# Three projection parts of a tenth set of later tokens move from the segments to the front of a one-core transformer kernel, with its instruction order searched anew

## The chip, the cores and the metric

The kernel runs on one core of a Trainium2 chip. Its engines are TensorE (PE, whose weight loads are listed apart as PEld), VectorE (DVE), ScalarE (ACT), GpSimd (POOL) and SyncE (SP), which issues most of the DMA transfers. The metric is device time in microseconds (us), the median of several runs.

## What is computed

A residual block with two halves, over 2048 tokens of width 640. The first half goes through the tokens in 64 segments of 32. Each segment sees 8 memory rows and its 32 tokens, has 32 heads of width 128, and its first 8 output rows are the memory of the next segment, so segments depend on each other in a chain:

```python
for s in range(n_seg):                       # 64 segments
    h = concatenate([mem, xs], axis=1)       # 8 memory rows + 32 tokens
    q, k, v = h @ Wq, h @ Wk, h @ Wv         # 640 -> 32 heads x 128
    p = softmax(where(mask, q @ k.T * scale, -1e9))
    o = (p @ v) @ Wo                         # 4096 -> 640
    mem = o[:, :M]                           # memory of the next segment
    outs.append(o[:, M:])
h = x + attention(layernorm(x))
out = h + ((relu(g) * u) @ W_down)           # g, u = layernorm(h) @ W_gate, W_up; 1728 wide
```

## The kernel before

**Rows of a segment.** The chain needs 32 rows at a time: 8 of memory and the segment's first 24 tokens. The last 8 tokens of a segment do not depend on memory before attention. They are called the later tokens here (`rest` in the code). They are projected ahead, for four segments at once: 32 rows make a *set*, so there are 16 sets, numbered from 0. A set has six *parts*: Q and K of the first 16 heads, Q and K of the other 16, and V of each half, in the order Q0, K0, Q1, K1, V0, V1. A part is 20 matmuls of 128x512 into one PSUM bank (5 chunks of the contraction, 4 column groups; L1577). Its bank is copied out by ACT (L1411) or DVE (L1412); Q and K are turned by DVE (L1599), K is rearranged by POOL as well (L1604); the result is stored to DRAM (`scr_qk`, L1607; `scr_v`, L1624), and a segment later loads what it needs (`RS`, L1640 and L1644).

**Where the later tokens come from.** Sixteen segments' later tokens, four sets, are loaded, normalized and transposed together (`ln1r`, L1526). Sets 0 to 3 use buffer `xr0`, sets 4 to 7 `xr1`, sets 8 to 11 `xr0` again, filled by a transposing DMA on SP's queue (L1532).

**Stages.** In the first stage Wq, Wk, Wv and Wo are loaded, while PE projects `EARLY` = 9 whole sets and the first segment. Then come the segments. In the gaps of the chain PE does work that is not urgent: the parts of the remaining sets, the output projection of the later tokens (`ro`, L1661), and gate and up projections of the feed-forward part (`gx`, L1742). Last comes the rest of the feed-forward part.

`RATES` says how many parts the segments get: an entry (s0, s1, count) spreads `count` parts over the segments from s0 up to s1. `EXTRA` says how many parts of set number `EARLY` are made in the first stage, with no segment to wait for. The code exists before the change too, with `EXTRA` at 0:

```python
for part in range(EXTRA):
    rest(EARLY, part)
...
for n in range(base + cnt * (s - s0) // (s1 - s0), base + cnt * (s - s0 + 1) // (s1 - s0)):
    z, part = divmod(n + EXTRA, 6)
    z += EARLY
    if z >= NQ:
        break
    rest(z, part, go)
```

In the segments a part also waits for the memory rows of its segment (`go`). Sets from number 8 on use two PSUM banks (4 and 5) and store through SP; the sets before them use all eight and store through ACT. Sets from number 9 on have three staging tiles.

**The order.** The order of each engine's instructions is not written by hand. Each operation is entered with an estimated duration, its dependencies and its buffers. When the kernel is built, a list scheduler (`_Sched.schedule`, L964) plays the program through, and takes, of the operations that can start about now, the one with the highest priority. The priority is the length of the work that follows, plus an entry of the table `BIAS` (L28), by name and by name and segment. The table `ENGINE` (L682) fixes which of ACT and DVE does a copy. Both tables are the result of a search over the scheduler's own model. The instructions then run in this order on each engine, and wait for each other with semaphores. Wherever an engine stands, everything behind it stands too.

**Names that the steps use.** L1577 is every projection (rows `xT` are a segment's own, rows `xr` the later tokens'). L1691 transposes a segment's input rows, of which the memory rows come last: it marks the start of a segment. L1954 and L1958 are scores, L1968 and L1555 sums of the softmax, L1993 and L1998 the product with V, L2027 and L2046 the output projection of the memory rows, L1963 to L1980 the softmax on ACT and DVE, L1497 a normalization, L2076 the turn of a segment's own Q and K, L1778 and L1834 the feed-forward part.

Of the kernel before, what the change touches and what calls it, by code (L numbers as in the profile page):

```python
# [18 lines left out]
RATES = ((1, 20, 32), (20, 50, 10))  # L19
EXTRA = 0  # L20
# [7 lines left out]
BIAS = {"sel2": -428.53, "ezero": 827.13, "ldxs0": 772.6, "ldxs1": -1075.19, "ldxa": 977.15, "ldxl": -444.97,  # L28
    "ldxx": 94.56, "ldxn": 296.11, "ldxx0": -425.81, "ldxst": -946.28, "ldxxm": -329.88, "ldmev": -440.02,
# [18 lines left out]
    "gx": -75.13, "gxrelu": -736.07, "gxev": -228.23, "gxst": -268.67, "ln2nd": -1166.07, "xnld": 1080.06,  # L48
    "gld": -294.56, "gu": 52.5, "relu": 1032.72, "gmul": -789.51, "roz": -16.73, "tn2go": 142.03,
# [1214 lines left out]
def build_kernel(nc, A_x, A_mem0, A_Wq, A_Wk, A_Wv, A_Wo, A_seg_len, B_x, B_W_gate, B_W_up,  # L1264
# [46 lines left out]
    sel2 = ar.alloc("sel2", [128, 64], BF16)  # L1311
# [21 lines left out]
    oTr = [ar.alloc(f"oTr{i}", [128, H, 32], BF16) for i in range(2)]  # L1333
# [547 lines left out]
    for nm, b in (("ldxr", 9000.0), ("ldxr1", 8950.0)):  # L1881
        for t in ("", "s0", "s1", "a", "l", "x", "n", "T", "e"):
            sc.bias[nm + t] = b
# [369 lines left out]
```

## Time and profile before

| | us |
|---|---|
| median of 3 runs | 998.24 |
| lowest and highest run | 994.87, 998.29 |
| profiled execution | 995.62 |
| its span, first to last instruction | 993.9 |

The mean granted clock of TensorE in the profiled execution was 0.998. By the rows of the profile: 21 MB of weights come in during the first stage, each load of Wq, Wk and Wv 512 KB and of Wo 640 KB. The segments last from about 87 us to 874 us, a little over 12 us each.

How to read it: the page gives busy time by engine, the chain of work that ended last, and groups of instructions by line. A row of a group has line, engine, operation, output<-input, shapes and count; then busy time and mean duration in ns; then the idle time of the engine just before and what ended it. A row of the timeline has start and length in us, and in brackets the idle time before it and its releaser. `ps` is a PSUM bank, `stg` and `tok` are staging tiles.

### The profile page before, as it was taken

How to read it: one execution, taken by the hardware profiler on the slowest of the kernel's cores; microseconds unless marked ns; L12 is line 12 of the kernel's file. 1: busy time of each engine (PE TensorE's matmuls, PEld its weight loads, DVE VectorE, ACT ScalarE, POOL GpSimd, SP SyncE). 2: the span in 40 equal slices, each digit the busy share in tenths (PEclk: the TensorE clock that was granted, in tenths of full speed). 3: DMA queues.
4: the chain of work that ended last, by engine and by line, in shares of the span. 5: the costliest groups of instructions: out<-in, count | busy, mean ns of one | idle time of the engine just before them, and what ended most of it. 6: DMA issues, size and time to landing. Idle time of an engine off the chain costs nothing.

```text
span 993.9 us, 54620 instructions
## 1 busy us (share of the span) xinstructions
PE 973.8 (98%) x25518; PEld 535.7 (54%) x24540; DVE 618.3 (62%) x1345; ACT 502.4 (51%) x1226; POOL 112.5 (11%) x264
## 2 busy tenths in 40 slices
PE   7989999999999999999999999999999999999998
PEld 4334565555555555655555556555555565543343
DVE  5835767768676766576666676767656766523232
ACT  2236555556565565555555565555555656521020
POOL 2341011111011011001000010000100000100000
PEclk9999999999999999999999999999999999999999
DMA  8996122223131323232232234333223352289211
GB/s 320 403 350 145 45 57 57 66 53 92 36 89 39 85 76 83 55 81 66 67 84 62 78 105 86 86 93 79 52 72 89 76 102 76 68 260 288 72 41 40
DMA packets 181553, 103.62 MB, mean 104 GB/s; under 512 B 126212, under 2 KB 177484, under 8 KB 181324
## 3 DMA queue, kind: packets, MB, share of 16 engines
q1 hardware_dynamic: 175948, 95.51, 34.5%
q10 hardware_dynamic: 5376, 4.63, 1.4%
q8 instruction: 196, 3.21, 1.3%
q14 instruction: 33, 0.27, 0.1%
HBM read 67.30 MB, written 29.75 MB: 98 GB/s over the span
## 4 chain that ended last, share of the span: by engine, by line
PE 90%; DMA 4%; SPq 3%; DVE 1%; issue 1%; ACT 0%; POOL 0%; ACTq 0%; DVEq 0%; POOLq 0%
PE ps L1577 49%; PE ps L2046 7%; PE ps L1742 7%; PE ps L2027 7%; PE ps L1834 4%; PE ps L1661 3%; PE ps L1778 3%; PE ps L1993 3%; DMA scr_qk<-stg 3%; PE ps L1555 2%; PE ps L1968 2%; PE ps L1954 1%; SPq L2164 1%; DMA Wq<-in_A_Wq_dram 1%; DMA scr_o<-osr 1%
## 5 line engine op out<-in xcount | busy, mean ns | idle before, releaser
L1411 ACT ACTIVATE tok<-ps 128x512 bf16<-128x512 f32 x216 | 128.2, 597 | 146.5 <-PE ps L1577 141.4
L1577 PE MATMUL ps<-Wk,xT 128*32 128x512 bf16 x2560 | 180.4, 379 | 0.4 <-ACT tok L1411 0.4
L1577 PE MATMUL ps<-Wv,xT 128*32 128x512 bf16 x2560 | 176.3, 379 | 0.0
L1577 PE MATMUL ps<-Wq,xT 128*32 128x512 bf16 x2560 | 170.1, 379 | 0.5 <-DVE tok L1412 0.3
L2076 DVE STREAM_TRANSPOSE QT<-tok 128x512 bf16<-128x512 bf16 x128 | 90.6, 708 | 47.5 <-ACT tok L1411 45.4
L1577 PEld LDWEIGHTS ps<-Wq,xT 128*32 128x32 bf16 x2560 | 70.6, 97 | 66.5 <-DVE xT L1691 9.1
L2076 DVE STREAM_TRANSPOSE KT<-tok 128x512 bf16<-128x512 bf16 x128 | 90.8, 709 | 24.6 <-ACT tok L1411 22.7
L1577 PEld LDWEIGHTS ps<-Wk,xT 128*32 128x32 bf16 x2560 | 68.4, 96 | 55.6 <-DVE xT L1691 2.9
L1963 ACT ACTIVATE E<-ps 128x224 bf16<-128x224 f32 x128 | 45.7, 357 | 81.4 <-PE ps L1958 77.7
L2046 PE MATMUL ps<-Wo,oT 128*32 128x160 bf16 x4096 | 83.5, 233 | 1.0 <-issue 1.0
L2046 PEld LDWEIGHTS ps<-Wo,oT 128*32 128x32 bf16 x4096 | 74.1, 97 | 15.5 <-ACT oT L1411 5.6
L2027 PE MATMUL ps<-Wo,oT 128*32 128x320 bf16 x2048 | 81.5, 300 | 0.9 <-DVE oT L1412 0.8
L1577 PEld LDWEIGHTS ps<-Wv,xT 128*32 128x32 bf16 x2560 | 61.0, 96 | 38.8 <-ACT tok L1411 0.7
L1412 DVE CAST oT<-ps 128x320 bf16<-128x320 f32 x124 | 55.0, 485 | 42.9 <-PE ps L1998 36.9
L1940 POOL COPY QT<-RS 128x256 bf16<-128x256 bf16 x64 | 25.7, 402 | 470.4 <-PE ps L1958 470.2
L1411 ACT ACTIVATE Vm<-ps 128x512 bf16<-128x512 f32 x122 | 72.0, 591 | 11.4 <-PE ps L1577 6.3
L1412 DVE CAST tok<-ps 128x512 bf16<-128x512 f32 x104 | 68.7, 661 | 9.6 <-PE ps L1577 9.3
L2027 PEld LDWEIGHTS ps<-Wo,oT 128*32 128x32 bf16 x2048 | 52.7, 96 | 27.3 <-DVE oT L1412 7.7
L1688 DVE CAST_PREDICATED xm<-turn,ps 128x64 bf16<-128x64 uint16 x126 | 27.9, 222 | 61.3 <-PE ps L1555 61.1
L2011 POOL COPY oTr<-oT 128x128 bf16<-128x128 bf16 x128 | 41.0, 320 | 193.5 <-ACT oT L1411 110.4
L1411 ACT ACTIVATE oT<-ps 128x320 bf16<-128x320 f32 x132 | 50.4, 436 | 11.5 <-PE ps L1998 11.1
L1411 ACT ACTIVATE ps<-seed 128x384 f32<-128x384 bf16 x117 | 54.4, 489 | 2.1 <-DVE half L2035 1.8
(108 smaller groups left out, 1453.5 us busy)
## 6 DMA issues: line engine op xcount, KB each, us to landing
RS<-scr_qk SPq DMA_DIRECT2D x63, 128.0 KB, 2.3
big<-in_A_x_dram SPq DMA_DIRECT2D x34, 160.0 KB, 2.8
Wq<-in_A_Wq_dram SPq DMA_DIRECT2D x10, 512.0 KB, 7.7
Wk<-in_A_Wk_dram SPq DMA_DIRECT2D x10, 512.0 KB, 8.2
Wv<-in_A_Wv_dram SPq DMA_DIRECT2D x10, 512.0 KB, 8.6
Wo<-in_A_Wo_dram SPq DMA_DIRECT2D x8, 640.0 KB, 11.2
Wgs<-in_B_W_gate_dram SPq DMA_DIRECT2D x30, 160.0 KB, 3.0
Wus<-in_B_W_up_dram SPq DMA_DIRECT2D x30, 160.0 KB, 2.9
```

What stands on the lines that cost most here:

```text
L1411: return e.activation(dst, src, ACTF.Copy)
L1412: return e.tensor_copy(dst, src)
L1577: o = pe.matmul(out, lhs[c], rhs, start=(c == 0), stop=(c == DC - 1), skip_group_check=True)
L1661: o = pe.matmul(bank(bk)[p0:p0 + 32, 0:2 * SLICE], oTr[b][:, h, :], cols(h, 2 * a, 2 * a + 2), start=(h < 2), stop=(h >= H - 2), skip_grou ...
L1742: o = pe.matmul(bank(bk)[32 * i:32 * i + 32, 0:512], wt[:, c, 32 * i:32 * i + 32], xn2T[0][:, :, c * 128:(c + 1) * 128], start=(c == 0), s ...
L1778: o = pe.matmul(bank(bk)[:, 0:TB], lhs(c), xT[:, :, c * 128:(c + 1) * 128], start=(c == 0), stop=(c == DC - 1))
L1834: pe.matmul(bank(ba)[:, 0:512], lhs, Wd[:, j, 0:512], start=(j == 0), stop=(j == FC - 1), skip_group_check=True)
L1963: op("act", lambda a: a.activation(E[:, g, :, 0:56], sco(BS[g]), ACTF.Exp, scale=SCALE), r=["table"], w=[("E", g)], x=[BS[g]], dur=0.36, n ...
L2011: op("pool", lambda e: e.tensor_copy(oTr[ob][:, 16 * g:16 * g + 16, XR * y:XR * y + XR], oT[:, 16 * g:16 * g + 16, 0:XR]), r=[("oT", g, 0) ...
L2027: o = pe.matmul(bank(BA)[p0:p0 + 32, 0:2 * SLICE], oT[:, h, XR:40], cols(h, 2 * b2, 2 * b2 + 2), start=(i == 0 and jj < 2), stop=(i == 3 a ...
L2046: o = pe.matmul(bank(BW)[32 * j:32 * j + 32, 0:SLICE], oT[:, 16 + 4 * jj + i, XR:40], cols(h, j, j + 1), start=(i == 0 and jj == 0), stop= ...
L2076: op("dve", lambda v, tb=tb, dst=dst: v.transpose(dst, tok[tb.at][:, :].rearrange("p (h r) -> p h r", r=32)), w=[("QT" if p == 0 else "KT" ...
```

## The change

```diff
-RATES = ((1, 20, 32), (20, 50, 10))
-EXTRA = 0
+RATES = ((1, 20, 30), (20, 50, 9))
+EXTRA = 3
...
-BIAS = {"sel2": -428.53, "ezero": 827.13, "ldxs0": 772.6, "ldxs1": -1075.19, "ldxa": 977.15, "ldxl": -444.97,
+BIAS = {"sel2": -751.1, "ezero": 242.82, "ldxrs0": 9232.52, "ldxrs1": 9076.28, "ldxra": 9061.94,
...
-ENGINE = {"ldxre": "act", "ldxr1e": "act", "ldmev": "act", "er0ev": "dve", "er0Tev": "act", "er1ev": "act",
+ENGINE = {"ldxre": "act", "ldmev": "act", "er0ev": "dve", "er0Tev": "act", "er1ev": "act", "ervev": "act",
...
     for nm, b in (("ldxr", 9000.0), ("ldxr1", 8950.0)):
         for t in ("", "s0", "s1", "a", "l", "x", "n", "T", "e"):
-            sc.bias[nm + t] = b
+            sc.bias[nm + t] = BIAS.get(nm + t, b)
```

Three parts of set 9 (Q0, K0 and Q1) are entered with the first stage and wait for no segment. The segments get 39 parts instead of 42. The tables `BIAS` and `ENGINE` are replaced as a whole (of the shared names of `BIAS` none keeps its value), and the first two normalizations of later tokens (`ldxr`, `ldxr1`) may now have entries of their own in place of fixed priorities. No operation is added or removed.

More of the change, by code (lines that the diff above doesn't have):

```diff
@@ L27 @@
 FPIECES = ((512, 896), (896, 1664), (0, 512))
-BIAS = {"sel2": -428.53, "ezero": 827.13, "ldxs0": 772.6, "ldxs1": -1075.19, "ldxa": 977.15, "ldxl": -444.97,
-    "ldxx": 94.56, "ldxn": 296.11, "ldxx0": -425.81, "ldxst": -946.28, "ldxxm": -329.88, "ldmev": -440.02,
[18 rows of a table removed]
-    "gx": -75.13, "gxrelu": -736.07, "gxev": -228.23, "gxst": -268.67, "ln2nd": -1166.07, "xnld": 1080.06,
-    "gld": -294.56, "gu": 52.5, "relu": 1032.72, "gmul": -789.51, "roz": -16.73, "tn2go": 142.03,
[632 rows of a table removed]
-ENGINE = {"ldxre": "act", "ldxr1e": "act", "ldmev": "act", "er0ev": "dve", "er0Tev": "act", "er1ev": "act",
-    "ervev": "act", "r0ev": "dve", "r0Tev": "act", "r1ev": "act", "rvev": "dve", "Q0ev": "act", "Q0Tev": "act",
-    "K0ev": "act", "K0Tev": "act", "V0ev": "act", "Q1ev": "dve", "Q1Tev": "dve", "K1ev": "act", "K1Tev": "act",
-    "seed0": "act", "seed1": "act", "oTev0": "dve", "oTev1": "act", "osrev": "act", "ldxre@0": "act",
[81 rows of a table removed]
+BIAS = {"sel2": -751.1, "ezero": 242.82, "ldxrs0": 9232.52, "ldxrs1": 9076.28, "ldxra": 9061.94,
+    "ldxrl": 8743.99, "ldxrx": 9122.57, "ldxrn": 9501.8, "ldxrT": 8472.55, "ldxre": 8973.64, "ldxs0": 717.86,
+    "ldxs1": -1637.42, "ldxa": 1163.05, "ldxl": -124.32, "ldxx": 287.42, "ldxn": -278.49, "ldxx0": -348.56,
[4 rows of a table added]
+    "eord": -1683.57, "er2mm": -1519.25, "ervev": 350.89, "ervdma": -307.94, "ln1r": 1207.68,
[16 rows of a table added]
+    "gxst": -478.48, "ln2nd": -1192.12, "xnld": 969.32, "gld": -114.25, "gu": -47.31, "relu": 754.04,
+    "gmul": -128.97, "roz": 72.23, "tn2go": 411.24, "tn2lx": -1087.89, "tn2lo": -2119.48, "tn2h": -120.28,
+    "tn2hd": 320.17, "tn2s0": -549.71, "tn2s1": -389.35, "tn2a": -100.62, "tn2l": 1131.52, "tn2x": -650.59,
+    "tn2n": -1065.29, "tn2nd": 918.93, "hld": 842.75, "down": -514.08, "hadd": -455.68, "outdma": -1014.75,
[631 rows of a table added]
+ENGINE = {"ldxre": "act", "ldmev": "act", "er0ev": "dve", "er0Tev": "act", "er1ev": "act", "ervev": "act",
+    "r0ev": "dve", "r0Tev": "act", "r1ev": "act", "rvev": "dve", "Q0Tev": "act", "K0ev": "act", "K0Tev": "act",
+    "Q1ev": "dve", "Q1Tev": "dve", "K1ev": "act", "K1Tev": "act", "seed0": "act", "seed1": "act",
+    "oTev0": "dve", "oTev1": "act", "osrev": "act", "gxrelu": "dve", "ldxr1e@0": "act", "er1ev@-1": "act",
[89 rows of a table added]
 class _Slot:
```

1471 rows, old and new, of tables (BIAS, ENGINE) are left out of this document.

## The prediction

> **What bounds the kernel now.** I read the page's busy shares first, then its chain of work that ended last, then the busy time by stage. The row after the shares is the chain by engine.
>
> ```profile
> span 993.9 us, 54620 instructions
> ...
> PE 973.8 (98%) x25518; PEld 535.7 (54%) x24540; DVE 618.3 (62%) x1345; ACT 502.4 (51%) x1226; POOL 112.5 (11%) x264
> ...
> PE 90%; DMA 4%; SPq 3%; DVE 1%; issue 1%; ACT 0%; POOL 0%; ACTq 0%; DVEq 0%; POOLq 0%
> ```
>
> The profiled execution took 995.62 us: its span of 993.9 and 1.7 around it. That is 2.6 under the median of the runs shown (998.24), so what I work out in its time is added to both. The view of windows gives three stages (columns: stretch, length, then busy time and count of each engine, granted clock, DMA share, GB/s):
>
> ```profile
> 0.00:87.00 87.00, 75.15 (x1524) 35.91 (x1516) 49.23 (x93) 31.96 (x72) 26.80 (x54) 0.98 0.98 332
> 87.00:863.00 776.00, 772.81 (x22892) 446.56 (x22140) 525.79 (x1173) 448.66 (x1110) 82.88 (x204) 1.00 0.29 73
> 863.00:994.00 131.00, 125.89 (x1122) 53.22 (x890) 43.26 (x80) 21.79 (x45) 2.78 (x6) 1.00 0.46 140
> ```
>
> Up to 87 us the DMA engines are full (0.98) and PE has 12 us of idle time; from 87 to 863, the segments, PE is idle for 3; after 863, the feed-forward part, for 5. A busy PE is a modelled thing, so I tested whether it is the bound. The first row below is a run of 176 projection matmuls without a break; the last four are whole segments, cut where a segment's input rows are transposed (L1691); PE's count of matmuls stands behind its busy time.
>
> ```profile
> 58.65 9.88 PE L1577 MATMUL ps<-Wv,xr 128*32 128x512 bf16 x176
> ```
>
> ```profile
> 776.53:788.44 11.91, 11.89 (x364) 6.49 (x344) 9.69 (x25) 8.23 (x21) 1.11 (x3) 1.00 0.34 91
> 662.12:674.28 12.16, 12.16 (x368) 6.88 (x352) 8.24 (x19) 6.53 (x16) 0.99 (x3) 1.00 0.26 68
> 711.38:724.62 13.24, 13.24 (x388) 7.43 (x372) 8.96 (x19) 6.54 (x16) 0.99 (x3) 1.00 0.31 73
> 186.01:199.46 13.45, 13.45 (x388) 7.10 (x372) 9.10 (x19) 7.65 (x18) 0.99 (x3) 1.00 0.24 60
> ```
>
> One matmul of this shape costs (9.88 - 0.38)/175 = 0.0543 us, its own 0.38 (a mean of 379 ns in the groups of the page) being the pipeline's length. A segment with 388 matmuls is 1.08 longer than one with 368, which is 20 times 0.0543. A segment with 364 is again 0.25 shorter. So from 13.45 down to 11.91 a segment lasts as long as PE has matmuls to issue, and no latency of the recurrence shows yet. That is the main reading: in the segments a matmul taken away is time taken away.
>
> **The change part by part.**
>
> *Three parts leave the segments.* A part of a set is 20 matmuls (5 chunks of the contraction by 4 column groups): 20 x 0.0543 = 1.09 us. Segments 1 to 19 get 30 parts instead of 32, segments 20 to 49 get 9 instead of 10, so 3 x 1.09 = **-3.26 us**. This holds while the segments that lose one stay above the shortest that the rows show, 11.91. Most have two fill-ins or more, so I take the whole of it; the bounds are -3.26 and 0, which is what it is if the latency of a segment appears just below 11.9.
>
> *Three parts come to the front.* They are the same 60 matmuls, three evictions and their turns, now without a segment to wait for. The work moves and stays the same in sum: an eviction on ACT or DVE, a transposition on DVE, one rearrangement on POOL (only one of the three, the K part) and three stores.
>
> ```profile
> L1599 DVE STREAM_TRANSPOSE stg<-tok 128x512 bf16<-128x512 bf16 x34 | 23.1, 699 | 8.0 <-ACT tok L1411 3.3 <-DMA scr_qk<-stg 2.9 <-POOL RS L1612 0.7
> ...
> L1604 POOL COPY stg<-stg 128x512 bf16<-128x512 bf16 x16 | 17.7, 1105 | 13.2 <-DVE stg L1599 11.2 <-DMA scr_qk<-stg 1.4
> L1412 DVE CAST tok<-ps 128x512 bf16<-128x512 f32 x19 | 12.5, 659 | 5.6 <-PE ps L1577 5.6
> ```
>
> So 3 x 0.66 and 3 x 0.70 on DVE, 1.1 on POOL: engines at 62% and 11%. PE's own work beside them hides them; without that cover the three evictions with their turns would be 4.1 us of DVE. What matters is when they may start. The tenth set reads the same later tokens as the ninth, in xr0, and these come from one transposing DMA on SP's queue:
>
> ```profile
> L1532 SPq DMA_TRANSPOSE xr<-big x1: 1339/1339/1339, 70.9 to 70.9; - x1
> ...
> DMA to landing us min/median/max: 4.8/4.8/4.8
> ```
>
> They are in place at 70.9 + 4.8 = 75.7. "During the load" is thus its very end: the first matmul of the ninth set is the 78.24 row below, and the first segment ends at 87.8. What room has PE there?
>
> ```profile
> 70.07 0.25 PE L1968 MATMUL ps<-E,bones 128*32 128x160 bf16 x4 [1.55 <-ACT E L1963]
> 70.15 0.20 PE L1555 MATMUL ps<-E,bones 128*32 128x64 bf16 x4
> 70.75 2.12 PE L1577 MATMUL ps<-Wv,xr 128*32 128x512 bf16 x20 [0.39 <-ACT lnS L1976]
> 73.45 4.95 PE L1577 MATMUL ps<-Wv,xr 128*32 128x512 bf16 x80 [0.58 <-ACT stg L1411]
> 78.24 1.25 PE L1577 MATMUL ps<-Wq,xr 128*32 128x512 bf16 x20
> 80.29 1.05 PE L1577 MATMUL ps<-Wq,xr 128*32 128x512 bf16 x16 [0.80 <-DVE tok L1412]
> ...
> 81.97 0.25 PE L1968 MATMUL ps<-E,bones 128*32 128x160 bf16 x4 [0.28 <-ACT E L1963]
> ...
> 82.45 0.27 PE L1993 MATMUL ps<-E,Vm 32*128 32x40 bf16 x16 [0.21 <-ACT stg L1411]
> ```
>
> ```profile
> L1577 PE MATMUL ps<-Wk,xr 128*32 128x512 bf16 x40 | 2.7, 381 | 0.0
> L1577 PE MATMUL ps<-Wq,xr 128*32 128x512 bf16 x40 | 2.6, 380 | 0.8 <-DVE tok L1412 0.8
> L2046 PE MATMUL ps<-Wo,oT 128*32 128x160 bf16 x64 | 1.3, 233 | 0.0
> L2027 PE MATMUL ps<-Wo,oT 128*32 128x320 bf16 x32 | 1.3, 300 | 0.1
> ```
>
> The second fence groups PE's work from 78.24 to 87.81. The idle time that the rows name there is 0.80 + 0.28 + 0.21 = 1.29 us. At most it is 9.57 less the 80 projection matmuls (4.34) and the two output projections (1.3 each): 2.63, with attention's short matmuls still to be taken off. I take 2.0, the middle: so much of the 3.26 is hidden, and **+1.26** stays. Bounds: 0 if all is hidden, +3.26 if none is. An extra part also needs one of two PSUM banks and three staging tiles, and the 0.80 wait is for such an eviction; that is why I don't count on more.
>
> *Queues.* The ninth and later sets store through SP, in order with the loads that segments 1 to 3 need:
>
> ```profile
> 81.01 0.35 SPq L1607 DMA_DIRECT2D scr_qk<-stg  x1
> ```
>
> Three more cost 3 x 0.35 = 1.1 us of SP's time there and save as much later. No new wait is written; but an extra matmul that stands too early in PE's order waits for the tokens, and the first segment's scores, value products and output projections wait behind it, then every later segment. I price that at nothing, with 1.1 as the upper end.
>
> *The order.* Of the bias table's 3645 entries (then 3638) 3199 names are shared and none keeps its value; of 260 shared engine choices 58 change. No row can tell what that gives. The rows bound it: two segments of 388 matmuls last 13.24 and 13.45, so an order's luck is worth about 0.2 us in a segment, either way, and in 62 segments such luck averages out to some +-3 us. I take 0. The feed-forward part keeps its work, and its 5.1 us of idle are the most that a new order can win there. Bounds of 5 either way; I take 0, and +-2 as likely.
>
> **Sum:** -3.26 + 1.26 + 0 = -2.0 us: 993.6 in the profiled execution's time, **996.2** as a median.
>
> *A rule against this.* The Trainium skill's page Perfetto Trace Analysis (section Identifying the Most-Contended Engine) says that matmul busy share does not tell how near PE is to its limit, and that the share of weight loads does. By that, PE has room (its weight loads are at 54%), the three parts cost nothing where they are, and the sum would be 0 or +1.26. The equal steps of the segment rows speak against it here; it supports the second case below.
>
> **The rivals.**
>
> *The gain of the segments is not there, or is paid in front (998.2).* Either a segment's latency begins just under 11.9, or the extra parts find no room before segment 1 and run in segments 1 to 3 in place of others: -3.26 + 3.26 = 0. For it: the tokens land at 75.7, with four of the ninth set's six parts already filling the gaps. Against it: 1.29 us of named idle time.
>
> *The hole of the load closes as well (990.7).* From 69 to 75 us PE waits (1.55, 0.39, 0.58) and runs slowly. The granted clock, the third number from the right, is 0.66 of full over 5 us:
>
> ```profile
> 70.00:75.00 5.00, 3.95 (x48) 1.26 (x48) 1.06 (x3) 2.86 (x9) 0.00 (x0) 0.66 1.15 261
> ```
>
> ```profile
> 70.47 0.45 DVE L1497 TENSOR_SCALAR big<-big,mv,rstd 128x640 bf16<-128x640 bf16 x1 [9.58 <-ACT rstd L1491]
> ```
>
> The later tokens' normalization stands 9.58 us waiting for ACT. If the new order brings it forward, the ninth and tenth sets fill the hole: 2.52 of waits and 5 x 0.34 = 1.7 for the clock are 4.2, the 1.26 is hidden too, and the change is -2.0 - 1.26 - 4.2 = -7.5. Against it: the waits are for ACT and staging with DMA full, which earlier tokens do not mend. The skill's page TensorE: Matmul & The Clock Gate (Part 1) has the clock halve after an idle window of about 3.4 us. Here it falls behind gaps of 1.55 and 0.39, so the trace does not bear that length out; a shorter hole need not spare the clock.
>
> *The new order makes each segment longer (1005.5).* Place: the evictions between projections, scores and output, where an eviction on the other engine ends later and its transposition with it. Price: 62 us for each us per segment. With 0.15 more it is +9.3 - 2.0 = +7.3. It outweighs the -2.0 from 0.03 per segment, and makes the kernel slower by 0.5% from (5.0 + 2.0)/62 = 0.11. For it: segment 1 lasts 13.15 with 368 matmuls, a whole 1.0 over the 12.16 above, so an order can cost that much:
>
> ```profile
> 87.42:100.57 13.15, 12.35 (x368) 6.86 (x352) 7.43 (x16) 7.94 (x19) 3.79 (x7) 1.00 0.42 106
> ```
>
> Against it: of the segments shown no other has an excess of over 0.2.
>
> **How the numbers follow.** Forecast (996.2): 0.43. Nothing gained (998.2): 0.17. Hole closed (990.7): 0.23. Longer segments (1005.5): 0.17. The order's +-3 and the feed-forward's +-2 lie around each of them. The range from 989 to 1004 leaves out the better part of the hole's case and the worse half of the slower one, about 2 in 10 together. A measurement of this kernel can tell about 0.5% from no change, 5.0 us, as the runs before spread over 3.4. Faster by more (under 993.2): most of the hole's case and a tail of the forecast, 0.30. Slower by more (over 1003.2): most of the last case, 0.16, with 0.01 from the others: 0.17. Within: 0.53.
>
> **What would show it.**
>
> ```profile
> L1691 DVE STREAM_TRANSPOSE xT<-xm x128: 202/252/281, 25.8 to 862.5; 128x96 bf16<-128x96 bf16 x64, 128x64 bf16<-128x64 bf16 x64
> ```
>
> Right: the memory transposition of segment 1 stays within 2 us of 87.4 with some three parts more done before it, and the stretch from it to the last one (862.5 now) shrinks by about 3. Second case: that stretch shrinks by 3 and its start moves back by 3, or neither moves. Third: a granted clock of 1.0 near 72, and a start of segment 1 at 84 or earlier. Fourth: segments of 368 matmuls that last 12.3 or more. What would make me wrong altogether is an idle gap of several us at a place where there is none now, in the feed-forward part above all, on which nothing here bears.

## The result, and the profile after

The changed kernel takes 1006.9 us as a median of 5 runs (1006.09 to 1008.0), the kernel before 998.29 on the same chip (994.87 to 1001.28 in 5 runs). The ratio is 1.0086, with a 95% interval of 1.0069 to 1.0104: slower by 6.9 to 10.4 us. The forecast was 996.2, with a range up to 1004. Of the runs further down, one execution of b_move (1956.58 us) and one of f_tail (1037.2 us) were slow and are left out of the ratios.

The profiled execution took 1007.13 us with a span of 1005.4, against 995.62 and 993.9. The page's busy shares hardly moved:

```profile
span 1005.4 us, 54620 instructions
...
PE 978.9 (97%) x25518; PEld 536.5 (53%) x24540; DVE 625.5 (62%) x1352; ACT 495.6 (49%) x1219; POOL 110.8 (11%) x264
```

The 11.5 us between the spans are cut at the same two marks as in the prediction, the input transposition of segment 1 (first row: a view of that line in a window) and the last one (second row: of the whole run). The code line L1691 is now L1704; every line behind the tables is 13 lower.

```profile
L1704 DVE STREAM_TRANSPOSE xT<-xm x2: 245/262/279, 91.2 to 91.6; 128x64 bf16<-128x64 bf16 x1, 128x96 bf16<-128x96 bf16 x1
```

```profile
L1704 DVE STREAM_TRANSPOSE xT<-xm x128: 203/262/280, 22.6 to 869.6; 128x96 bf16<-128x96 bf16 x64, 128x64 bf16<-128x64 bf16 x64
```

Segment 1 starts at 91.2 in place of 87.4 (**front +3.8**). From there to the last transposition it is 778.4 and not 775.1 (**segments +3.3**). From 869.6 to the end it is 135.8 and not 131.4 (**tail +4.4**). All three stages lost. Part of it is idle time of PE: by the view of windows 9.1 us from 25 us to segment 1 in place of 5.7, 4.2 in the segments in place of 3.2, and 8.5 in the tail in place of 5.0. The split is that of two executions. The tail also holds a little less work than before: 64 matmuls of the later tokens' output projection stand behind the last transposition and not 128 (some 2 us), against 26 gate and up projections of the segments' kind in place of 4 (1.2 us).

How many parts of the later tokens run ahead of segment 1? The view of the projection line up to 91.21 us gives (count behind the names):

```profile
L1590 PE MATMUL ps<-Wq,xr x360: 377/379/634, 10.5 to 85.1; 128*32 128x512 bf16 x180
L1590 PE MATMUL ps<-Wk,xr x360: 379/379/390, 36.1 to 91.2; 128*32 128x512 bf16 x180
L1590 PE MATMUL ps<-Wv,xr x320: 377/379/634, 56.8 to 81.8; 128*32 128x512 bf16 x160
```

Nine sets have 2 x 20 matmuls with Wq each, 360 in all. So the Q parts of set 9 are not among them. The three rows give 1040 / 20 = 52.0 parts; in the kernel before it was 360, 356 and 320 up to 87.42, which is 51.8. So next to nothing left the segments: of the 1920 matmuls of the later tokens they hold 880, and 884 before. The next Q part starts at 127 us, in segment 3, and in the kernel before at 108 (timeline, after and then before; start, length):

```profile
127.15 0.39 PE L1590 MATMUL ps<-Wq,xr 128*32 128x512 bf16 x4
```

```profile
108.29 0.60 PE L1577 MATMUL ps<-Wq,xr 128*32 128x512 bf16 x8
```

The next K part starts at 124.59 (before: 123.04). The three parts that were entered with the first stage run in the segments after all, and Q0 and Q1 later than before.

In the front PE now waits at places where it did not wait before (timeline, idle time and releaser in brackets):

```profile
62.19 6.66 PE L1590 MATMUL ps<-Wv,xr 128*32 128x512 bf16 x120 [1.76 <-ACT stg L1424]
71.97 0.28 PE L1967 MATMUL ps<-QT,KT 128*32 128x40 bf16 x16 [3.12 <-POOL QT L1953]
...
82.03 1.25 PE L1590 MATMUL ps<-Wq,xr 128*32 128x512 bf16 x20
```

The scores of segment 0 (L1967) stand 3.12 us for a copy by POOL, and set 8 begins at 82.03 and not at 78.24. The clock falls behind these waits to 0.74 and then 0.92 (third number from the right); in the kernel before it was 0.66 from 70 to 75:

```profile
70.00:75.00 5.00, 3.03 (x52) 1.34 (x56) 0.45 (x1) 1.83 (x5) 0.99 (x3) 0.74 0.49 147
75.00:80.00 5.00, 4.60 (x87) 2.06 (x76) 1.94 (x5) 3.67 (x10) 0.00 (x0) 0.92 0.63 133
```

In the tail the down projection waits 2.28 us for an addition on DVE, and 1.1 us after that wait its matmuls of 512 columns begin to last 0.59 to 0.63 in place of 0.38:

```profile
928.02 0.39 PE L1847 MATMUL ps<-Wd,gTs 128*128 128x512 bf16 x1 [2.28 <-DVE tl L1854]
...
929.12 0.59 PE L1847 MATMUL ps<-Wd,gTs 128*128 128x512 bf16 x1
```

### The profile page after: what moved, and what is told of

The parts are those of the page before. It is cut to its first block, busy times and chain, and to the rows that moved or that the text cites. A ratio compares the mean times of both kernels' runs of the same rounds, so it can differ in the third digit from the quotient of the medians.

```text
span 1005.4 us, 54620 instructions
## 1 busy us (share of the span) xinstructions
PE 978.9 (97%) x25518; PEld 536.5 (53%) x24540; DVE 625.5 (62%) x1352; ACT 495.6 (49%) x1219; POOL 110.8 (11%) x264
## 4 chain that ended last, share of the span: by engine, by line
PE 87%; DMA 2%; SPq 1%; DVE 1%; issue 0%; ACT 0%; POOL 0%; DVEq 0%; POOLq 0%
PE ps L1590 46%; PE ps L2059 7%; PE ps L2040 7%; PE ps L1755 7%; PE ps L1791 5%; PE ps L1674 3%; PE ps L1847 3%; PE ps L2006 3%; PE ps L1568 2%; PE ps L1981 2%; PE ps L1967 1%; DMA scr_o<-osr 1%; SPq L1688 0%; PE ps L1971 0%; PE ps L2076 0%
## 5 line engine op out<-in xcount | busy, mean ns | idle before, releaser
L1424 ACT ACTIVATE tok<-ps 128x512 bf16<-128x512 f32 x223 | 132.2, 597 | 135.2 <-PE ps L1590 128.3
L1590 PE MATMUL ps<-Wq,xT 128*32 128x512 bf16 x2560 | 168.0, 379 | 0.3 <-DVE xT L1704 0.3
L2089 DVE STREAM_TRANSPOSE QT<-tok 128x512 bf16<-128x512 bf16 x128 | 90.5, 708 | 41.3 <-ACT tok L1424 39.1
L1425 DVE CAST tok<-ps 128x512 bf16<-128x512 f32 x97 | 64.0, 660 | 7.7 <-PE ps L1590 7.6
```

Source lines behind the costliest of these rows:

```text
L1424: return e.activation(dst, src, ACTF.Copy)
L1425: return e.tensor_copy(dst, src)
L1590: o = pe.matmul(out, lhs[c], rhs, start=(c == 0), stop=(c == DC - 1), skip_group_check=True)
L2089: op("dve", lambda v, tb=tb, dst=dst: v.transpose(dst, tok[tb.at][:, :].rearrange("p (h r) -> p h r", r=32)), w=[("QT" if p == 0 else "KT" ...
```

## The experiments

Two questions were asked. Are the terms of the prediction right, apart from the new order (p_alone, o_alone, b_cut, b_move, b_less, b_more)? And what in the new order costs the 11.5 us (all others)? At first there were three theories. A: the two numbers are worth about nothing and the loss is the new order's. B: the sum of the prediction is right and the order hides it. C: the two numbers themselves make it slower.

Medians of the kernel before differ by chip (997 to 1001.5), so ratios to it on the same chip are compared. The last three columns are the profiled execution's: start of segment 1, from there to the last transposition, from there to the end. One execution fixes them only to some us: after and f_same have the same order, and their segments take 778.4 and 782.9.

| run | median | ratio, interval | segment 1 | segments | tail |
|---|---|---|---|---|---|
| before | 998.29 | 1 | 87.4 | 775.1 | 131.4 |
| after | 1006.90 | 1.0086 [1.0069, 1.0104] | 91.2 | 778.4 | 135.8 |
| p_alone | 1023.14 | 1.0258 [1.0241, 1.0275] | 87.6 | 795.0 | 136.9 |
| o_alone | 1022.52 | 1.0249 [1.0231, 1.0267] | 91.7 | 797.2 | 132.8 |
| b_cut | 1001.36 | 1.0019 [1.0003, 1.0036] | 87.5 | 779.5 | 132.2 |
| b_move | 1002.39 | 1.0026 [1.0010, 1.0041] | 92.1 | 776.9 | 131.0 |
| b_less | 1000.03 | 0.9999 [0.9988, 1.0011] | 88.7 | 777.1 | 131.8 |
| b_more | 1005.44 | 1.0068 [1.0051, 1.0085] | 88.2 | 782.4 | 132.1 |
| f_rstd_b | 999.64 | 1.0006 [0.9990, 1.0022] | 87.4 | 777.7 | 130.5 |
| f_same | 1009.65 | 1.0093 [1.0070, 1.0116] | 91.2 | 782.9 | 133.8 |
| f_front | 1009.21 | 1.0095 [1.0074, 1.0115] | 91.0 | 782.4 | 134.1 |
| f_rstd | 1009.91 | 1.0103 [1.0086, 1.0121] | 91.7 | 782.6 | 132.9 |
| f_tail | 1016.37 | 1.0156 [1.0131, 1.0182] | 91.0 | 782.1 | 138.4 |
| f_tail2 | 1010.00 | 1.0089 [1.0069, 1.0108] | 91.8 | 781.3 | 133.9 |
| f_all | 1010.90 | 1.0091 [1.0063, 1.0120] | 91.4 | 784.5 | 135.7 |
| a_odma | 1011.85 | 1.0147 [1.0133, 1.0162] | 90.8 | 778.9 | 140.1 |
| a_front | 1005.79 | 1.0085 [1.0068, 1.0102] | 91.0 | 780.2 | 135.5 |
| a_tail | 1019.64 | 1.0182 [1.0157, 1.0206] | 90.5 | 782.2 | 145.2 |
| a_both | 1019.22 | 1.0174 [1.0152, 1.0196] | 87.6 | 785.2 | 145.6 |

### Each half of the change alone

```diff
# p_alone: before, with its own tables
-RATES = ((1, 20, 32), (20, 50, 10))
-EXTRA = 0
+RATES = ((1, 20, 30), (20, 50, 9))
+EXTRA = 3
# o_alone: after, with these two lines as before
```

> The kernel before with the new RATES and EXTRA and its own old tables. Theory A (the two numbers are worth nothing, because the three parts of set 9 do not run before segment 1 but behind set 8, in segments 1 to 3; all of the loss is the new order): within 2 us of the 998.3 of before, and 52 parts done when segment 1 starts, as in both profiles. Theory B (the prediction's sum is right, and the new order hides it): 996.3, and 54 to 55 parts done by then. Theory C (fewer parts to fill the segments lets them wait, or the extra parts crowd the first segments): 1002 or more.

> The changed kernel with the old RATES and EXTRA, that is, the new tables alone. Theory A: as slow as the changed kernel, 1007 within 2 us. Theory B: 1009, since the gain of the two numbers goes. Theory C: 1003 or less, since the loss of the two numbers goes.

Each half alone costs 2.5%, some 25 us; together they cost 0.86%. None of the three theories had that. A table belongs to one program: with three parts entered elsewhere, the old entries order the segments badly, and so do the new entries with the old parts; most of the loss is in the segments (795.0 and 797.2). So the two numbers can't be judged apart from a table, and "0" was no neutral guess for the order. In p_alone segment 1 starts at 87.6 with 51.8 parts before it, as in the kernel before: the old table does not place the extra parts there either. The two halves can't be told apart in this way, hence the next four, which keep the order of before on every engine.

### Matmuls taken away and added in a fixed order

```diff
# b_cut: five parts in the segments; b_move: also parts 0 to 2 of set 8
-                    for j in range(4):
+                    for j in js(c):
# c is the chunk, j the column group
# b_cut:  js = 4 column groups in chunk 0, one in the other four
# b_move: b_cut, and in the front chunk 0 issued 6 times
# b_less: ten parts, as b_cut, and those single matmuls on 32 columns
# b_more: the same ten parts, chunk 0 issued 4 times
```

> The kernel before with its own order, in which five fill-in parts of the segments (the third part of sets 10, 11, 12, 13 and 15) issue 8 matmuls in place of 20: 60 matmuls less, so those parts of the projection are not computed in full. Everything else stands where it stood. It measures the first term of the prediction by itself. If matmul issue bounds the segments, as the prediction read: 60 x 0.0543 = 3.26 less, about 0.3% under the kernel before. If a segment's latency bounds them (the rival, and the rule on weight loads): no change, within 0.5 us.

b_cut is a miss of its design. It was 0.19% slower, but its parts were no shorter. In the same segment, four matmuls of a segment's own V (four column groups) and the last four of a cut part (one column group):

```profile
244.02 0.39 PE L1577 MATMUL ps<-Wv,xT 128*32 128x512 bf16 x4
...
248.33 1.03 PE L1577 MATMUL ps<-Wq,xr 128*32 128x512 bf16 x4
```

Four matmuls of four column groups take 0.39 together. Four of one group take 1.03, (1.03 - 0.38)/3 = 0.217 for each step, which is four times 0.0543. The four groups run side by side; with three of them left out the fourth takes as long. So b_cut tests nothing of the first term. It is told because 0.0543 is a rate of four groups together, and not the price of a matmul.

> As b_cut, and with the 60 matmuls put back in the front: parts 0, 1 and 2 of set 8 issue their first four matmuls six times over, 20 more each, between 78 and 88 us. This is the change's matmul count moved within the order of before. By the prediction's sum (-3.26, +1.26): 2.0 under the kernel before. If the gaps there hide nothing: the same as before (0). If the segments gain nothing: 1.3 to 3.3 over it.

As b_cut's parts are no shorter, b_move is b_cut with 60 matmuls added. From the first matmul of set 8 to segment 1 it is 12.16 us in b_move (79.94 to 92.10) and 9.18 before (78.24 to 87.42): 2.98 more, of the 3.26 that 60 matmuls cost. Next to nothing of them is hidden in the front; the prediction's 2.0 was not there. The other 1.7 by which segment 1 starts later lie ahead of set 8. In the medians b_move is only 0.07% over b_cut, less than the noise of either (their intervals are 0.15 to 0.17% each way), so this reading rests on two traces.

> The kernel before with its own order, in which ten fill-in parts of the segments (the first and third of sets 10 to 14, each in another segment) issue their first four matmuls in full and, for the other four chunks, one matmul of 32 columns in place of four of 512: those parts of the projection are not computed in full. Here, other than in b_cut, all four column groups get less to do: a part lasts about 0.4 us in place of 1.09, ten parts 6 to 7 us less. If matmul time bounds the segments (the first term of the prediction): 6 to 7 under the kernel before. If latency bounds them (the rule on weight loads): within 1 of it. If the order is tuned to the old lengths and every change of them brings waits: 0 to 3 over it.

> The kernel before with its own order, in which the same ten parts issue their first four matmuls four times over: 120 matmuls more, 120 x 0.0543 = 6.5 us. The other sign of b_less. If matmul time bounds the segments: 6 to 7 over the kernel before. If latency bounds them: within 1. If the order is tuned to the old lengths: 7 to 10 over.

These two decide, and neither theory had both. b_less is as fast as the kernel before, within 1.2 us either way, where 6 to 7 us less were due. b_more is 5.1 to 8.5 us slower, where 6.5 were due. Segments 7 and 8, in the view of windows, before, b_less and b_more:

```profile
161.54:173.84 12.30, 12.13 (x364) 6.83 (x352) 9.58 (x22) 7.62 (x19) 2.22 (x4) 1.00 0.27 78
173.84:186.01 12.17, 12.17 (x368) 6.91 (x348) 8.92 (x21) 7.73 (x20) 2.08 (x4) 1.00 0.31 82
```

```profile
163.35:175.64 12.29, 12.10 (x356) 6.71 (x340) 9.58 (x22) 7.83 (x20) 2.22 (x4) 1.00 0.28 78
175.64:187.56 11.92, 11.38 (x344) 6.47 (x332) 8.92 (x20) 7.63 (x20) 2.09 (x4) 1.00 0.33 83
```

```profile
163.01:175.96 12.95, 12.78 (x376) 7.23 (x364) 9.58 (x22) 7.62 (x19) 2.22 (x4) 1.00 0.29 82
175.96:188.78 12.82, 12.82 (x380) 7.24 (x360) 8.92 (x21) 7.73 (x20) 2.08 (x4) 1.00 0.28 74
```

With 12 matmuls more, each segment is 0.65 longer, to the digit 12 x 0.0543. With fewer, one is 0.01 shorter and the other 0.25. The segment of 13.45 that the prediction read as 388 matmuls long (186.01:199.46) is 13.23 in b_less, 0.22 shorter where 0.65 was due:

```profile
187.56:200.79 13.23, 12.72 (x370) 7.00 (x358) 9.11 (x19) 7.65 (x18) 0.99 (x3) 1.00 0.25 60
```

Over all segments, in the same order of before, b_less and b_more, PE's idle time (length less PE's busy time) is 3.19, 8.66 and 4.13:

```profile
87.42:862.50 775.08, 771.89 (x22872) 446.07 (x22124) 525.18 (x1171) 448.16 (x1109) 82.88 (x204) 1.00 0.29 73
```

```profile
88.66:865.78 777.12, 768.46 (x22752) 449.45 (x22004) 524.84 (x1170) 448.36 (x1109) 83.13 (x204) 1.00 0.30 72
```

```profile
88.24:870.67 782.43, 778.30 (x22992) 449.68 (x22244) 525.37 (x1170) 448.51 (x1109) 83.00 (x204) 1.00 0.29 72
```

Of the idle time in b_less 4.9 us are waits for copies and transpositions of the chain (tiles oT, xT and Vm), and 1.7 before. Where the time stays is seen at the end of segment 13, on PE, from the last sum of a segment to the first projection of the next (before, then b_less):

```profile
247.60 0.24 PE L1555 MATMUL ps<-half,sel 128*32 128x160 bf16 x4
247.67 1.04 PE L1577 MATMUL ps<-Wq,xr 128*32 128x512 bf16 x16
248.53 0.60 PE L1577 MATMUL ps<-Wq,xT 128*32 128x512 bf16 x8
```

```profile
249.99 0.30 PE L1555 MATMUL ps<-half,sel 128*32 128x160 bf16 x4
250.06 0.26 PE L1577 MATMUL ps<-Wq,xr 128*32 128x32 bf16 x4
250.88 0.61 PE L1577 MATMUL ps<-Wq,xT 128*32 128x512 bf16 x8 [0.57 <-DVE xT L1691]
```

From sum to projection it is 0.93 before and 0.89 in b_less. Before, the fill-in ends just when the new memory rows have been copied and transposed on DVE. Without it PE waits 0.57 for that transposition. (As a whole this segment is 0.86 longer in b_less, since PE also stands 0.79 at 249.69 for nothing that the profile shows.) **The fill-ins that were cut are about as long as the waits of the recurrence.** That is why no wait shows in the profile of before, and why it may not be read as "PE bounds this".

### Single waits of the new order, moved one at a time

For these the program's order is worked out as before, kept as a list for each engine, and only the operations named are set elsewhere in it. Semaphores are derived anew. f_same moves nothing, and is the changed kernel again: 1.0093.

```diff
+class _Fixed(_Sched):
+    def schedule(self):
...
+        super().schedule()          # the order, and each buffer's place
...
+        seq = moved(seq)            # what an experiment moves
+        for k, o in enumerate(seq): # dependencies and waits anew, in this order
...
-    sc = _Sched()
+    sc = _Fixed()
# f_front: set 0 and set 3 change places in K0 and K1; POOL's copies of set 0's K
#          and into QT stand among the K rearrangements, not behind them
# f_rstd:  ln1rl, ln1rx, ln1rn (later tokens) ahead of set 0's K stores; ln1rT ahead of segment 1's load
# f_rstd_b: the same in the kernel before, there ahead of the first V eviction of set 1
# f_tail:  the stores odma of the last segment and ordma of the last set ahead of the loads hld
# f_tail2: odma of the last segment alone, ahead of the feed-forward weights' third load of Wg
# f_all:   f_front, f_rstd (there ahead of the second V eviction of set 0) and f_tail2
```

> The changed kernel with its order frozen and nothing moved: the same instructions in the same order on every engine. It is the base for the other frozen kernels, on the same chip. Every theory expects the changed kernel's time, 0.8 to 0.9% over the kernel before.

> The changed kernel with its order frozen, but set 0 and set 3 change places in their K parts (same shapes, same places), and GpSimd's two copies of them and its copy into QT stand where they can be had, some 10 us earlier. If the front's loss is the 3.12 us wait of segment 0's scores for that copy, with the clock that falls behind it (about 1.5): 4 to 5 less than the changed kernel, about 1002, and segment 1 starts at 87. If another wait is as late: 0 to 1 less, as when the front's table entries of before were put back.

The wait went and nothing was gained: segment 1 at 91.0. The timelines of POOL and ACT in the changed kernel, and of POOL, PE and ACT in f_front, show why:

```profile
71.51 0.40 POOL L1953 COPY QT<-RS 128x256 bf16<-128x256 bf16 x1 [0.17 <-POOLq L1944]
```

```profile
73.33 0.36 ACT L1976 ACTIVATE E<-ps 128x224 bf16<-128x224 f32 x1 [0.87 <-issue]
```

```profile
58.06 0.40 POOL L1953 COPY QT<-RS 128x256 bf16<-128x256 bf16 x1 [0.17 <-POOLq L1944]
```

```profile
67.21 0.27 PE L1967 MATMUL ps<-QT,KT 128*32 128x40 bf16 x16
...
70.96 4.46 PE L1590 MATMUL ps<-Wv,xr 128*32 128x512 bf16 x40 [3.44 <-ACT stg L1424]
```

```profile
70.31 0.60 ACT L1424 ACTIVATE stg<-ps 128x512 bf16<-128x512 f32 x1 [4.24 <-DMA scr_qk<-stg]
...
72.68 0.36 ACT L1976 ACTIVATE E<-ps 128x224 bf16<-128x224 f32 x1 [1.29 <-issue]
```

The copy into QT is 13.4 us earlier (71.51 to 58.06), the scores 4.8. But ACT stands 4.24 us for a staging tile that a store must release, and the exponential of these scores is behind that eviction in ACT's order: 72.68, 0.65 earlier than in the changed kernel (73.33). PE's wait of 3.12 has become one of 3.44.

> The changed kernel with its order frozen, but for the normalization of the later tokens of sets 8 to 11: its two short instructions on ScalarE stand ahead of the stores of set 0 and not behind segment 0's exponential, and its transposing load stands ahead of segment 1's on SP. The theory: five stores of V stand behind that transposition on SP's queue (74.61, then 76.12), the staging tiles of the evictions wait for them, and segment 1 starts 16.6 us after the transposition in both kernels. Then it goes at 66 to 67, the stores at 71.5, and segment 1 starts 3 to 4 us earlier: 1003. Rival: the weights' load, or segment 0's wait for the copy into QT, is as late: 0 to 1 less than the changed kernel.

> The same move in the kernel before, order otherwise frozen: the transposition of the later tokens at 66 to 67 and not at 70.9, the stores of V 1 to 2 us earlier. By the theory: 1 to 2 under the kernel before, with segment 1 at 86. Rival: no change.

SP's queue in the changed kernel, then in f_rstd:

```profile
74.61 1.34 SPq L1545 DMA_TRANSPOSE xr<-big  x1
76.12 3.41 SPq L1637 DMA_DIRECT2D scr_v<-stg  x5
```

```profile
67.75 1.34 SPq L1545 DMA_TRANSPOSE xr<-big  x1
...
71.15 7.23 SPq L1637 DMA_DIRECT2D scr_v<-stg  x5
```

The transposition went 6.9 us earlier as meant, but the five stores behind it take 7.2 us in place of 3.4 to be issued, and segment 1 starts at 91.7. In the kernel before the move changed nothing either. The transposition stands 16.5 us ahead of segment 1 in both kernels, but segment 1 does not follow it when it is moved.

> The moves of f_front, f_rstd and f_tail2 together. If each of the front's waits only hides the next, and taking two of them away frees the third: segment 1 starts at 87 to 88 and the kernel is 6 to 8 us faster than f_same, level with the kernel before. If the front is held by what the three have in common (staging tiles that stores release only when the weights' load lets them land): segment 1 stays at 91, and only f_tail2's gain shows.

Two of the front's waits removed together leave segment 1 at 91.4. So neither these waits alone nor both make the front's loss. Up to 70 us the DMA engines are full in both kernels, and staging tiles come back only as stores land; that this is the common limit is an inference, and what sets 91 rather than 87 was not found by moving single instructions.

> The changed kernel with its order frozen as it is, but for three stores on SP's queue: the last segment's output rows and the last set's later rows now stand ahead of the loads of h for the feed-forward part, some four places earlier. No other engine's order changes. If the tail's 2.28 us wait behind the normalization and the half clock after it come from that late store: 3 to 4 less than the changed kernel, about 1003. If something else is as late there: 1006 to 1007.

> The same, with one instruction moved: the store of the last segment's output rows stands on SP behind the first four loads of feed-forward weights, some sixteen places earlier, and not behind the loads of h. So nothing waits for its landing at the head of the queue, as the loads of g did in f_tail. If the late store is what the tail waits for: the wait of 2.28 us behind the normalization and the half clock after it go, 3 to 4 us less than f_same. If something else is as late there: within 1 of it.

The theory missed both times: f_tail is slower than either forecast, and f_tail2 within 1 us of f_same, as its rival said. SP and PE in f_tail:

```profile
909.08 1.26 SPq L1688 DMA_DIRECT2D scr_o<-osr  x2
...
912.30 0.43 SPq L1780 DMA_DIRECT2D gT<-scr_g  x1
```

```profile
916.98 0.61 PE L1847 MATMUL ps<-Wd,gT 128*128 128x512 bf16 x1 [5.73 <-DMA gT<-scr_g]
```

The stores of the later rows follow the last segment's store in the program and wait for it to land (issued at 904.51). Now they stood at the head of SP's queue with the load of g behind them, at 912.30, and PE waited 5.73 us for that (1.04 in f_same). In f_tail2 only the last segment's store moved, to 887.76 (909.40 in f_same), and the tail is 133.9 against 133.8:

```profile
887.76 0.53 SPq L2127 DMA_DIRECT2D scr_o<-osb  x1
...
911.17 5.32 SPq L1688 DMA_DIRECT2D scr_o<-osr  x2
...
925.16 0.45 SPq L1717 DMA_DIRECT2D big<-scr_o  x1
```

The next stores still take 5.3 us to issue and the load behind them goes at 925.16. The late store of the last segment alone was not the cause. PE's wait is still there (1.69 in f_same):

```profile
931.32 0.39 PE L1847 MATMUL ps<-Wd,gTs 128*128 128x512 bf16 x1 [2.38 <-DVE tl L1854]
```

### Entries of the tables put back

```diff
# a_odma: after, the last segment's store favoured
+BIAS.update({"odma@64": BIAS["odma@64"] + 3000.0})   # as a constant
# a_front: after, with before's entries of the first stage in BIAS and ENGINE
# a_tail:  after, with before's entries of the feed-forward stage
# a_both:  both
```

> The changed kernel with one entry of the table raised: the store of the last segment's output (scr_o<-osb) goes ahead on SP's queue, ahead of the feed-forward weights instead of behind them. In the changed kernel it is issued at 904.7 us, 21 us after it is ready; the later tokens' store, the last normalization on DVE and the additions behind that wait for it, PE stands 2.3 us at 925.7 and then runs at a lower clock for 3 us. Theory A (this late store is most of what the feed-forward part lost): 3 to 4 us less than the changed kernel, about 1003.5, no gap of PE near 926. Rival (another engine or load ends last there, and the gap only moves): 1006 to 1008.

> The changed kernel with all table entries that belong to the first stage alone (the early sets, the first normalizations, the setup) put back to those of before. Theory A (the front lost 3.8 us by its new order, and the segments keep that): segment 1 starts at about 87.5 instead of 91.2 and the time is 3 to 4 us less, about 1003. Rival (the start of segment 1 is set by the loads, and what is gained before it is waited for after): 1006 to 1008, with segment 1 starting earlier or not.

> The changed kernel, in which the entries of both tables that belong to the feed-forward part after the segments are those of before; the rest of the new tables stays, and the scheduler orders anew. If those entries make the tail longer (136.2 against 131.8 us): 3 to 5 less than the changed kernel, 0.4 to 0.5% over the kernel before. If the tail depends on how the segments leave the queues, or the entries fit only their own set: no gain, or slower.

> The same with the front's entries of before as well (those of a_front). If the entries of a stage make its time: 4 to 8 less than the changed kernel, 0 to 0.5% over the kernel before, and what stays is the segments' part. If a table fits only as a whole: as slow as the changed kernel, or slower.

None of the four gained clear of the noise. One raised entry (a_odma) takes the 2.28 us wait away, and PE's waits for the last weights and for g grow from 1.23 and 0.96 to 3.98 and 2.58: the tail is 4.3 longer. The old tail entries in the new order (a_tail) make it 9.4 longer, with a wait for weights that was in neither kernel:

```profile
902.12 4.45 PE L1791 MATMUL ps<-xn2T,Wg 128*128 128x512 bf16 x10 [5.95 <-DMA Wg<-in_B_W_gate_dram]
```

The front is another matter. a_front and a_both have the same order on every engine up to the last segments. In a_both segment 1 starts at 87.6, as in the kernel before, in a_front at 91.0. From 70 to 80 us, and the 80 or 100 matmuls that stand there, a_front and then a_both:

```profile
70.00:75.00 5.00, 2.12 (x36) 0.84 (x36) 1.78 (x5) 2.56 (x8) 0.00 (x0) 0.85 0.83 228
75.00:80.00 5.00, 5.00 (x56) 1.79 (x48) 0.60 (x1) 3.41 (x8) 0.00 (x0) 0.50 0.71 167
```

```profile
74.43 7.42 PE L1590 MATMUL ps<-Wv,xr 128*32 128x512 bf16 x80 [1.02 <-ACT stg L1424]
```

```profile
70.00:75.00 5.00, 3.94 (x48) 1.53 (x48) 2.02 (x6) 3.78 (x11) 0.00 (x0) 0.69 0.70 195
75.00:80.00 5.00, 4.68 (x84) 2.10 (x76) 0.63 (x2) 2.67 (x6) 0.00 (x0) 0.97 0.59 142
```

```profile
71.34 7.27 PE L1590 MATMUL ps<-Wv,xr 128*32 128x512 bf16 x100 [0.40 <-ACT lnS L1989]
```

With the old entries the front's 3.6 us come back in the a_both execution, and not in that of a_front, where the clock is at half for longer and a wait of 1.02 stands ahead of it. The times show no gain: a_front is at 1.0085 and after at 1.0086, a_both at 1.0174 and a_tail at 1.0182. The front's loss itself recurs: segment 1 starts at 90.5 to 91.8 in the six profiled executions with the changed kernel's front (after, f_same, f_tail, f_tail2, a_odma, a_tail), and at 87.4 to 88.7 in the four with that of before (before, b_cut, b_less, b_more). That it lies in the front's new entries as a whole is likely, but one execution of two does not show it.

## Why the prediction was wrong, step by step

**What bounds the segments: wrong.** "In the segments a matmul taken away is time taken away" failed. The equal steps between segments of 368 and 388 matmuls were right and showed what an added matmul costs (b_more: 0.65 for 12). They were read as if they held downwards too. b_less took twice as much away as the change was to take, and gained 0 with 1.2 either way. In the changed kernel itself the term was not even put to the test, as 880 matmuls of the later tokens stayed in the segments, of 884. The term of -3.26 is 0: its own other bound, "if the latency of a segment appears just below 11.9". In the segments that were cut the waits appeared near each one's own length (13.45 as well as 12.30), since the fill-ins fit its waits. The rule that was weighed there, of the Trainium skill's page Perfetto Trace Analysis (section Identifying the Most-Contended Engine), that matmul busy share does not show how near PE is to its limit, is borne out here by b_less for work taken away, and not by b_more for work added.

**"Three parts come to the front": wrong.** To enter them with the first stage did not make them run there. The new order placed them behind segment 1 (52.0 parts ahead of it against 51.8), so the +1.26 never arose, nor the 2.0 hidden. Had they come, b_move's trace says that they would have cost 2.98, near the upper bound of 3.26. Together with the first term, the two numbers come to about 0, as the rival "nothing gained" had it, and for a reason like the one that it named: the parts run in segment 3 and later, where it said 1 to 3. No run measures the two numbers by themselves, since with the old table they cost 25 us (p_alone).

**The order at 0 with some 3 either way: wrong, and the larger part.** With the two terms at 0, the whole +8.6 of the medians is left for it. The bound came from two segments of equal counts and from averaging over 62 of them. That misses what an order can do in the two other stages and that a table without its program costs 25 us (p_alone, o_alone). The fourth rival had the right sign with the wrong place: the segments took 3.3 us of 11.5 (f_same against f_rstd_b, two executions more: 5.2), 0.05 to 0.08 in each and not 0.15. Nor did each segment grow: the median of the 62 is 12.31 us before and 12.28 after.

**The feed-forward part at 0 with some 2 either way: too narrow** (+4.4, and +3.3 between f_same and f_rstd_b). What "would make me wrong altogether" is what came, if smaller: waits of 3.12 us in the front and 2.28 in that stage, where there were none.

**Queues: not put to the test.** Three stores more on SP ahead of segment 1 were priced at 1.1 us at most, but they went with their parts into the segments. What a store at the wrong place can cost, f_tail shows in the tail: a wait of 5.73 in place of 1.04.

Of the 11.5 us between the profiled executions 2.9 are theirs alone (before's is 2.7 under its median, after's 0.2 over). **Open** is which instructions of the new front and tail make the loss: no move in the frozen order made the front or the tail more than 1 us shorter than in f_same. Whether the new table was the best for the new numbers can't be told from these runs.

## What to carry to other kernels

A busy engine without waits is not yet a bound: where filler work was fitted into a chain's waits, adding cost in full and taking away gained nothing, so test both signs with the order kept fixed. A searched order has to be priced as a change of its own, by what a wait costs in every stage, and not by the spread between like segments. And when a wait is taken out of an in-order queue, look at once for the next instruction in that queue; here the wait came back at 3.44 for 3.12.

## What was not expected of the hardware

The clock fell to 0.50 for 5 us in a_front, behind waits of 1.61, 0.40 and 1.02 with work between, where a_both, in the same order, had 0.69 in the 5 us ahead and 0.97 in these: segment 1 starts 3.4 us apart, by luck. In the tail it fell 1.1 us after a wait of 2.28 had ended. The Trainium skill's page TensorE: Matmul & The Clock Gate (Part 1) ties the fall to an idle window of about 3.4 us; none of these waits is that long. Column groups of TensorE run side by side at 0.217 us for 512 columns, so leaving three of four out saves no time (b_cut).
